# List operands by nine token tiles, a routing in smaller parts, and scales copied on GpSimd

## The chip, the cores and the metric

The kernel runs on one core of a Trainium2 chip. The metric is the device time of one execution in microseconds (us); of several runs the median counts. Engines are called as the profile calls them: PE (TensorE matmul), PEld (its weight loads), DVE (VectorE), ACT (ScalarE), POOL (GpSimd) and SP (SyncE, which issues most DMAs).

## The reference

Attention over pooled queries feeds a mixture of eight experts, of which each token uses one.

```python
# q, k, v: 8 batches x 8 heads x 1152 x 64, float32
q_pool = q.reshape(B, H, S // 2, 2, D).mean(axis=3)          # 576 queries
scores = scale * np.matmul(q_pool, k.transpose(0, 1, 3, 2))
scores = scores - np.max(scores, axis=-1, keepdims=True)
attn = np.exp(scores)
attn = attn / (np.sum(attn, axis=-1, keepdims=True) + 1e-09)
x = np.matmul(attn, v)                                       # to 4608 tokens x 512
...
logits = x @ w_gate + modality_bias[modality_id]
e_idx = np.argmax(logits, axis=1)
gate_w = probs[np.arange(N), e_idx]                          # probs = softmax(logits)
for e in range(8):
    mask = e_idx == e
    out[mask] = gate_w[mask, None] * (np.maximum(x[mask] @ w1[e], 0) @ w2[e])
```

## The kernel before

**Attention** treats 32 pairs, numbered 0 to 31; a pair is one head of two neighbouring batches, and its two members are heads j = 0 and 1. A pair takes 18 steps, and the order of every engine's work is written out by hand: a loop over 576 steps calls small generators in a fixed order (`ORD`), `at` hangs a piece of work on a step, `later` puts it some steps on, and `later_end` puts it at a step's end. Every engine then works through its own list in that order and stops only where an operand is not there yet, so an engine may be ahead of the steps of the others.

The first half of a pair's work is done one or two pairs ahead:

- GpSimd pools the queries (`split_q`, line 603, tile `rawq`), casts them to float16 (line 610, `qh`) and takes three remainders (line 638, `lo`: the first of the queries, the other two of the keys, which wait for ScalarE's casts at line 622, `hi`).
- `maxpass` finds an upper bound of each query's scores: 18 matmuls of 512 columns and nine of 128 write to a pool of three PSUM tiles (`pm`, lines 771 and 779), and VectorE reduces each to one number per query (lines 772 and 780). A matmul of this kind can start only when the reduction of the tile three back is through.
- `square`, `power` and `scales` (lines 684 to 705) find a power of two from the values' sum of squares. `scales` runs at step 1 of the pair before: VectorE writes `half`, the two factors `sc`, and then the same number twice more, into the routing's `scales` and into `both` (line 698).
- GpSimd scales the values into `VH` in two pieces (line 725) at steps 3 and 4 of the pair before, VectorE makes the shifted copy `VS` (line 735) and the low parts `vl` (line 723).

The second half: `scores` makes the score matmuls (lines 833 and 834) and their exponentials on ScalarE (line 835, 24 for a pair). The lower halves of the exponentials' 32-bit words are turned into `Pl` (line 816 on ScalarE for two thirds, line 818 on VectorE for 576 columns); `pv` multiplies both by the values (lines 886 to 888). `evac` divides by the row sums (lines 904 to 909), and `split_x` (line 862) splits the result for the gate's logits, which odd pairs multiply (line 258).

**Routing.** After every eight pairs a quarter of the tokens (a group of nine tiles of 128) is complete. `route` then adds the logits up, finds the best expert and its probability, and counts by ten small matmuls how many tokens before this one chose the same expert. It is a generator that runs beside the attention: it is called once a step, and `yield n` lets it rest for n steps. `RS = 2` sets most of these rests.

**The first list.** When three groups are routed (in pair 26), `first_blocks`, `place` and `listing` sort their tokens into six blocks of 256, so that the experts can start as soon as the attention ends. `operands` builds, for three tiles of tokens at a time, a one-hot matrix of the lane (`ol`, line 471) and two products of a one-hot of the column (`o` at line 476, `r` at lines 478 and 479); nine matmuls for a group then write the list (line 498). In the pairs from `P_LIST` = 26 on, a third of VectorE's lower halves is done by ScalarE instead.

**Experts** come after pair 31, from about 754 us on: blocks of 256 tokens, w1 and w2 split into two float16 parts each, on PE without a break; the fourth group's routing and the second list run beside their first blocks.

Of the kernel before, what the change touches and what calls it, by code (L numbers as in the profile page):

```python
# [9 lines left out]
F32 = mybir.dt.float32  # L10
F32R = mybir.dt.float32r
F16 = mybir.dt.float16
BF16 = mybir.dt.bfloat16
# [9 lines left out]
P = 128  # L23
# [6 lines left out]
D = 64  # L30
# [12 lines left out]
T_LIST = -127  # L43
RS = 2
SLOW_P = 1
# [109 lines left out]
class Router:  # L155
# [11 lines left out]
    def setup(self, ids, w_gate, bias):  # L167
# [20 lines left out]
        nc.gpsimd.memset(self.on, 1.0)  # L188
        self.ie = self.iota("ie", E)
        self.lane16 = con.tile([P, P], BF16, name="lane16")  # L190
        nc.gpsimd.tensor_copy(self.lane16, self.iota("lane", P))
# [75 lines left out]
    def route(self, g, eng):  # L267

        nc, sm = self.nc, self.sm
        while self.added[g] < H // 2:  # L270
# [15 lines left out]
        yield RS + 1  # L286
# [3 lines left out]
        yield RS  # L290
# [6 lines left out]
        yield RS  # L297
# [5 lines left out]
        yield RS  # L303
        sx = sm.tile([P, NT], F32, name="sx")
        nc.vector.tensor_reduce(sx, w, op=ALU.add, axis=AX.X)
# [5 lines left out]
        nc.vector.reciprocal(ts2[:, 1:2], ts2[:, 0:1])  # L311
# [3 lines left out]
        eng.dma_start(out=self.xs[g * NT * P:(g + 1) * NT * P, DM:XW].rearrange("(t p) d -> p t d", p=P), in_=gt)  # L315
        yield RS
# [3 lines left out]
        nc.tensor.matmul(pr[:, 0:NT], self.up, oh16, start=True, stop=False, skip_group_check=True)  # L320
        for s in range(NT):
            nc.tensor.matmul(pr[:, s + 1:], self.on, oh16[:, s:s + 1].broadcast_to([P, NT - s, E]), start=False, stop=s == NT - 1,
                             skip_group_check=True)
# [5 lines left out]
        self.base = nb  # L329
        yield RS  # L330
        nc.gpsimd.tensor_tensor(pos, pos, oh, op=ALU.mult)
        yield RS
        nc.vector.tensor_reduce(self.pos[:, ts], pos, op=ALU.add, axis=AX.X)
# [29 lines left out]
    def first_blocks(self):  # L363

        nc, sm = self.nc, self.sm
        full = self.con.tile([P, E], F32, name="full")
        self.up_to(self.base, full)
        yield
        cum = self.running(full.unsqueeze(1), "cumA")[:, 0]
        yield  # L370
        left = sm.tile([P, E], F32, name="left")
        nc.vector.tensor_scalar(left, cum[:, 0:E], -1.0, float(NA), op0=ALU.mult, op1=ALU.add)
        nc.vector.tensor_single_scalar(left, left, 0.0, op=ALU.max)
        self.na = self.con.tile([P, E], F32, name="na")
        nc.vector.tensor_tensor(self.na, full, left, op=ALU.min)
        yield
        nc.vector.tensor_single_scalar(cum, cum, float(NA), op=ALU.min)
        self.cumA = cum
        yield
        self.ownA = self.owners(cum, NA, "A")  # L380

# [37 lines left out]
    def place(self, nt, late):  # L419
# [11 lines left out]
        def pick(o, of):  # L431

            nc.vector.tensor_tensor(w, oh, be(of), op=ALU.mult)
# [9 lines left out]
        if late:  # L443
            yield from pick(ok, self.done)
            nc.vector.tensor_tensor(ok, self.pos[:, 0:nt], ok, op=ALU.is_ge)
            more = new("more")
            yield from pick(more, self.half)
            nc.vector.tensor_tensor(more, more, ok, op=ALU.mult)
            nc.vector.tensor_tensor(row, row, more, op=ALU.add)
        yield  # L450
        nc.vector.tensor_tensor(ok, self.pos[:, 0:nt], lim, op=ALU.is_ge if late else ALU.is_lt)
# [4 lines left out]
        lo = sm.tile([P, NTT], I32, name="loi")[:, 0:nt]  # L456
        nc.vector.tensor_single_scalar(lo, ri, P - 1, op=ALU.bitwise_and)
        nc.vector.tensor_single_scalar(ri, ri, 7, op=ALU.logical_shift_right)
# [3 lines left out]
        nc.vector.tensor_copy(self.hi, ri)  # L462
        nc.vector.tensor_single_scalar(self.hi, self.hi, -float(2 * T // P), op=ALU.add)

    def operands(self, g, n, out):

        nc, sm = self.nc, self.sm
        for q in range(3):
            ts = slice(g * NT + 3 * q, g * NT + 3 * q + 3)
            ol = sm.tile([P, 3, P], BF16, name=f"ol{q}", bufs=1 + self.lag)  # L470
            nc.vector.tensor_tensor(ol, self.lo[:, ts].unsqueeze(2).broadcast_to([P, 3, P]), self.lane16.unsqueeze(1).broadcast_to([P, 3, P]),
                                    op=ALU.is_equal)
            yield SLOW
            o = sm.tile([P, 3, n], F32, name=f"o{n}")
            r = sm.tile([P, 3, 2, n], BF16, name=f"r{n}_{q}", bufs=1 + self.lag)
            nc.vector.tensor_tensor(o, self.hi[:, ts].unsqueeze(2).broadcast_to([P, 3, n]), self.col[:, 0:n].unsqueeze(1).broadcast_to([P, 3, n]),
                                    op=ALU.is_equal)
            nc.vector.tensor_tensor(r[:, :, 0], o, self.tile1[:, ts].unsqueeze(2).broadcast_to([P, 3, n]), op=ALU.mult)
            nc.vector.tensor_scalar(r[:, :, 1], o, self.part, None, op0=ALU.mult)
            out.append((ol, r))  # L480
            yield SLOW

    def listing(self, groups, n, acc):

        nc, ops = self.nc, []
        for g in range(groups + self.lag):
# [7 lines left out]
            if g >= 0:  # L494
                pm = self.pm(4)[:, 0:2 * n].rearrange("p (w n) -> p w n", w=2)
                for t in range(NT):
                    ol, r = ops[g][t // 3]
                    nc.tensor.matmul(pm, ol[:, t % 3], r[:, t % 3], start=t == 0, stop=t == NT - 1)
# [21 lines left out]
    def first_list(self):  # L520

        for _ in self.first_blocks():
            yield 2
        for _ in self.place(3 * NT, False):
            yield 2
        yield T_LIST
# [12 lines left out]
def attention(tc, ctx, att, ident, npairs, xpool, on_two, on_split, on_scale, jobs, side, set_pm, started, ahead, hip):  # L539
# [153 lines left out]
    def scales(p, pt):  # L693
# [102 lines left out]
    def scores(p, j, r):  # L796
# [9 lines left out]
        s["P", j, r] = (word(F16, 1), Pl, i % NR)  # L806
        lows = LOWS_LAST if p == npairs - 1 else LOWS_LIST if p >= P_LIST else LOWS if p else LOWS0
        lows = lows[i % len(lows)]
# [672 lines left out]
```

## Time and profile before

| | |
|---|---|
| time, median of 3 runs (lowest to highest) | 1164.33 us (1164.32 to 1165.66) |
| time of the profiled execution | 1162.89 us |
| its span, first to last instruction | 1161.2 us |
| granted TensorE clock, mean over the span | 0.996 |
| first exponential of pair 0, of pair 3, end of pair 31's last | 18.2, 100.5, 753.0 us |

The profile comes from one execution. Its page gives each engine's busy time. The view of windows gives the same for chosen stretches; the stretches used here begin and end where the first exponential of a pair starts, so one row is one pair. The timeline lists instructions in order of time: start and length in us, engine, line, operation, output<-input, and in square brackets how long the engine stood idle before it and what ended that. Neighbouring instructions of one kind are merged in a row (`x2`). A few per cent of the matmul records can be missing.

### The profile page before, as it was taken

Reading aid. Unit: us, or ns where it says so; the run is one execution under the profiler, and the core shown is the slowest. Engines: PE = TensorE matmul, PEld = TensorE weight load, DVE = VectorE, ACT = ScalarE, POOL = GpSimd, SP = SyncE. Lnnn points to the kernel's source line nnn. Section 1 sums busy time; section 2 is a strip of 40 time slices with the busy share of each in tenths; the row PEclk is TensorE's granted clock in tenths of the full one; section 3 lists DMA queues with packets and bytes.
Section 4 is the critical chain, followed back from the end, with each engine's and each line's share of the span. In section 5 each row is a group of like instructions: output and inputs, shape, how many; then the busy total and the mean of one; then the engine's idle time right before and its main releaser. Section 6 shows DMA issues by size and latency. Waiting matters only on the chain. (4 is left out here: it accounts for less than half of the span.)

```text
span 1161.2 us, 36622 instructions
## 1 busy us (share of the span) xinstructions
PE 1109.2 (96%) x14962; PEld 814.1 (70%) x14962; DVE 986.0 (85%) x2021; ACT 920.7 (79%) x1469; POOL 414.0 (36%) x394
## 2 busy tenths in 40 slices
PE   5989999999999999999999999999999999999995
PEld 2767777777777777777777677767676676766763
DVE  6888999999999999999999999788997667566671
ACT  5879999998999998999999999866566656565561
POOL 7843443444435344444443342123122121221201
PEclk9999999999999999999999999999999999999998
DMA  7667758767668668678678563599989999999970
GB/s 226 171 167 171 175 159 203 166 166 184 162 166 193 175 165 179 165 165 195 160 174 183 144 139 85 173 291 267 254 283 280 322 263 278 281 280 287 269 227 22
DMA packets 175569, 232.66 MB, mean 200 GB/s; under 512 B 92351, under 2 KB 126799, under 8 KB 175392
## 3 DMA queue, kind: packets, MB, share of 16 engines
q1 hardware_dynamic: 169254, 210.45, 70.3%
q0 software_dynamic: 6128, 19.78, 6.0%
q8 instruction: 119, 1.95, 0.7%
q14 instruction: 58, 0.48, 0.1%
q10 hardware_dynamic: 10, 0.00, 0.0%
HBM read 146.11 MB, written 19.18 MB: 142 GB/s over the span
## 5 line engine op out<-in xcount | busy, mean ns | idle before, releaser
L835 ACT ACTIVATE Pe<-psc 128x432 int32<-128x432 f32 x768 | 379.1, 526 | 51.7 <-PE psc L834 42.7
L772 DVE TENSOR_REDUCE mp<-pm 128x1 f32<-128x512 f32 x566 | 370.9, 683 | 18.4 <-PE pm L771 11.4
L886 PE MATMUL xp<-VH,Pe 128*128 128x65 f16 x2880 | 373.2, 193 | 0.0
L888 PE MATMUL xp<-VS,Pl 128*128 128x65 f16 x2880 | 372.5, 193 | 0.4 <-DVE Pl L818 0.4
L887 PE MATMUL xp<-vl,Pe 128*128 128x64 f16 x2880 | 371.2, 192 | 0.0
L887 PEld LDWEIGHTS <-Pe 128*128 128x128 f16 x2880 | 267.6, 98 | 87.8
L834 PE MATMUL psc<-B 65*128 65x432 f16 (+2 forms) x1152 | 305.6, 288 | 4.6 <-DMA B<-mr 4.3
L886 PEld LDWEIGHTS <-Pe 128*128 128x128 f16 x2880 | 272.1, 98 | 52.6 <-issue 15.3
L833 PE MATMUL psc<-B 128*128 128x432 f16 (+2 forms) x1152 | 305.0, 287 | 3.3 <-ACT Pe L835 3.0
L888 PEld LDWEIGHTS <-Pl 128*128 128x128 f16 x2880 | 266.5, 97 | 0.6 <-DVE Pl L818 0.5
L816 ACT ACTIVATE Pl<-Pe 128x1152 f16<-128x1152 uint16 x196 | 223.3, 1140 | 6.2
L771 PE MATMUL pm<-hi,QB 128*128 128x512 f16 x566 | 215.2, 382 | 11.7 <-DVE mp L772 8.3
L725 POOL TENSOR_SCALAR VH<-rawv,sc 128x512 f16<-128x512 f32 (+1 forms) x60 | 103.9, 1742 | 174.1 <-PE psc L834 72.8
L638 POOL TENSOR_TENSOR lo<-rawk,hi 128x576 f16<-128x576 f32 (+1 forms) x68 | 87.4, 1288 | 187.3 <-ACT hi L622 144.4
L1222 PE MATMUL ph<-xpart,w1l 128*128 128x256 f16 x544 | 148.3, 273 | 0.0
L1220 PE MATMUL ph<-xpart,w1h 128*128 128x256 f16 x544 | 148.3, 273 | 0.0
L1221 PE MATMUL ph<-xpart,w1h 128*128 128x256 f16 x544 | 148.3, 273 | 0.0
L834 PEld LDWEIGHTS <-B 65*128 65x128 f16 x1152 | 113.1, 98 | 28.6 <-issue 5.3
L833 PEld LDWEIGHTS <-B 128*128 128x128 f16 x1152 | 112.8, 98 | 8.2 <-issue 3.0
L1226 DVE SCALAR_TENSOR_TENSOR hl<-ph,hh 128x512 f16<-128x512 f32 x72 | 49.6, 689 | 74.5 <-ACT hh L1225 74.4
L1268 PE MATMUL po<-w2h,hl 128*128 128x512 f16 x296 | 112.2, 379 | 0.0
L1267 PE MATMUL po<-w2l,hh 128*128 128x512 f16 x296 | 112.2, 379 | 0.0
(264 smaller groups left out, 1843.3 us busy)
## 6 DMA issues: line engine op xcount, KB each, us to landing
w2r<-in_w_dram SPq DMA_DIRECT2D x76, 512.0 KB
w1r<-in_w_dram SPq DMA_DIRECT2D x72, 512.0 KB
rawv<-in_att_dram SPq DMA_DIRECT2D x32, 576.0 KB
B<-hi SPq DMA_DIRECT2D x128, 144.0 KB
rawq<-in_att_dram SPq DMA_DIRECT2D x31, 576.0 KB
rawk<-in_att_dram SPq DMA_DIRECT2D x31, 576.0 KB
B<-qh SPq DMA_DIRECT2D x128, 72.0 KB
B<-lo SPq DMA_DIRECT2D x64, 144.0 KB
```

What stands on the lines that cost most here:

```text
L771: nc.tensor.matmul(pm, QB[p % 2][:, u], s["hi"][:, t * 512:(t + 1) * 512], start=True, stop=True)
L772: nc.vector.tensor_reduce(mp[:, u, t:t + 1], pm, op=ALU.max, axis=AX.X)
L816: nc.scalar.activation(low, rest, AF.Copy, scale=LOW)
L833: nc.tensor.matmul(o, b1[:, ks], b1[:, qs], start=True, stop=False, skip_group_check=True)
L834: nc.tensor.matmul(o, b2[:, ks], b2[:, qs], start=False, stop=True, skip_group_check=True)
L835: nc.scalar.activation(Pe[:, D + x0:D + x1], pt, AF.Exp, scale=1.0 / 16)
L886: nc.tensor.matmul(out, Ph[:, qs], vh[:, c, j, 0:D + 1], start=c == 0 and g == 0, stop=False, skip_group_check=True)
L887: nc.tensor.matmul(out[:, 0:D], Ph[:, qs], vl[:, c, j], start=False, stop=False, skip_group_check=True)
L888: nc.tensor.matmul(out, Pl[:, qs], vs[:, c, j, 0:D + 1], start=False, stop=c == NKC - 1, skip_group_check=True)
L1220: nc.tensor.matmul(o, hi[:, c, fs], xh[:, :, c], start=c == 0, stop=False)
L1221: nc.tensor.matmul(o, hi[:, c, fs], xl[:, :, c], start=False, stop=False)
L1222: nc.tensor.matmul(o, lo[:, c, fs], xh[:, :, c], start=False, stop=c == 3)
```

## The change

- `scales` no longer writes `scales` and `both` on VectorE. A new function `keep`, one step later, copies them from `sc` on GpSimd.
- `route` is split into more parts. Its rests are four steps for the first two groups (`RS = (4, 4, 2, 2)`). Five of VectorE's operations for a group go: a compare and a cast are folded into their neighbours, and three small ones go to GpSimd.
- `first_blocks` is written out with a rest of one step after every operation or two, `place` has more rests and two operations fewer (three more in the second list).
- `operands` builds the column's one-hot and its two products for all nine tiles of a group at once, between the three lane matrices. A group's rests go from six to five.
- In pairs 28 to 30 all of the lower halves of 576 columns are VectorE's again (pairs 26 and 27 keep their third on ScalarE).

The core of the diff:

```diff
-RS = 2
+PL = 2
+RS = (4, 4, 2, 2)
...
-P_LIST = 26
-LOWS_LIST = (((0, 1152, 'A', 2), (1152, 1728, 'D', 3)), ((0, 1152, 'A', 2), (1152, 1728, 'D', 3)), ((0, 1152, 'A', 2), (1152, 1728, 'A', 3)))
+P_LIST = {26: 0, 27: 0}
+LOWS_LIST = [tuple(((0, 1152, 'A', 2), (1152, 1728, e, 3)) for e in x) for x in ('DDA', 'DA', 'A')]
...
         nc.scalar.activation(w, lg, AF.Exp)
-        nc.vector.tensor_single_scalar(w2, lg, 0.0, op=ALU.is_ge)
         key = big[1][:, 0]
-        nc.vector.scalar_tensor_tensor(key, w2, -float(E), be(self.ie), op0=ALU.mult, op1=ALU.add)
+        nc.vector.scalar_tensor_tensor(key, lg, 0.0, be(self.ieE), op0=ALU.is_ge, op1=ALU.mult)
...
-        oh = big[1][:, 1]
+        oh = sm.tile([P, NT, E], BF16, name="oh16")
         nc.vector.tensor_tensor(oh, key, bc(kmin), op=ALU.is_equal)
-        oh16 = sm.tile([P, NT, E], BF16, name="oh16")
-        nc.vector.tensor_copy(oh16, oh)
-        nc.vector.tensor_single_scalar(self.exp[:, ts], kmin, float(E), op=ALU.add)
-        yield RS
+        yield 1
+        nc.gpsimd.tensor_scalar(self.exp[:, ts], kmin, float(E), None, op0=ALU.add)
+        yield rs
         nc.vector.tensor_reduce(sx, w, op=ALU.add, axis=AX.X)
-        nc.vector.tensor_single_scalar(sx, sx, EPS, op=ALU.add)
...
-        nc.vector.tensor_single_scalar(ts2[:, 0:1], ts2[:, 0:1], 1.0 / XSC, op=ALU.mult)
+        yield 1
+        nc.gpsimd.tensor_scalar(sx, sx, EPS, None, op0=ALU.add)
+        nc.gpsimd.tensor_scalar(ts2[:, 0:1], ts2[:, 0:1], 1.0 / XSC, None, op0=ALU.mult)
+        yield 1
         nc.vector.reciprocal(ts2[:, 1:2], ts2[:, 0:1])
...
-            nc.vector.tensor_tensor(w, oh, be(of), op=ALU.mult)
+            nc.vector.scalar_tensor_tensor(w, oh, float(TB), be(of), op0=ALU.mult, op1=ALU.mult)
             yield
             nc.vector.tensor_reduce(o, w, op=ALU.add, axis=AX.X)
-            nc.vector.tensor_single_scalar(o, o, float(TB), op=ALU.mult)
...
     def operands(self, g, n, out):
-        for q in range(3):
...
-            yield SLOW
-            o = sm.tile([P, 3, n], F32, name=f"o{n}")
...
+        rows(0)
+        yield SLOW
+        o = sm.tile([P, NT, n], F32, name=f"o{n}")
+        nc.vector.tensor_tensor(o, self.hi[:, ts].unsqueeze(2).broadcast_to([P, NT, n]), self.col[:, 0:n].unsqueeze(1).broadcast_to([P, NT, n]),
+                                op=ALU.is_equal)
+        yield SLOW
+        rows(1)
+        yield SLOW
+        nc.vector.tensor_tensor(r[:, 0], o, self.tile1[:, ts].unsqueeze(2).broadcast_to([P, NT, n]), op=ALU.mult)
+        nc.vector.tensor_scalar(r[:, 1], o, self.part, None, op0=ALU.mult)
+        yield SLOW
+        rows(2)
+        yield SLOW
...
-        on_scale(p, lambda o: power_of(o, half, 1, 49))
         if p % 2 == 0:
             s["both"] = xpool.tile([P, 1], I32, name="both", bufs=3)
+        later(1, lambda: keep(p, sc))
+
+    def keep(p, sc):
+
+        on_scale(p, lambda o: nc.gpsimd.tensor_copy(o, sc[:, 1:2]))
         r = slice(p % 2 * D, (p % 2 + 1) * D)
-        power_of(st[p - p % 2]["both"][r], half[r], 1, 49)
+        nc.gpsimd.tensor_copy(st[p - p % 2]["both"][r], sc[r, 1:2])
```

Two places in the order of instructions. The first is GpSimd's list around the turn from one pair to the next, in the stretch before the first routing. Before, with the pooling (`rawq`) of the pair after next directly behind the last remainders (`lo`):

```order
L638 TENSOR_TENSOR lo<-rawk,hi 128x576 x2
L603 TENSOR_TENSOR rawq<-rawq 128x576
L725 TENSOR_SCALAR VH_125<-rawv,sc 128x8x64
L725 TENSOR_SCALAR VH_125<-rawv,sc 128x10x64
L610 CAST qh<-rawq 128x576
L638 TENSOR_TENSOR lo<-rawq,qh 128x576
```

The same stretch in the changed kernel, whose line numbers are larger by 30 to 34:

```order
L668 TENSOR_TENSOR lo<-rawk,hi 128x576 x2
L738 COPY scales<-sc 128x1
L740 COPY both<-sc 64x1
L633 TENSOR_TENSOR rawq<-rawq 128x576
L759 TENSOR_SCALAR VH_125<-rawv,sc 128x8x64
L759 TENSOR_SCALAR VH_125<-rawv,sc 128x10x64
L640 CAST qh<-rawq 128x576
L668 TENSOR_TENSOR lo<-rawq,qh 128x576
```

The two copies, which need `sc` of the running pair's step 1, now stand ahead of the pooling, and the pooling stays ahead of `VH`.

The second is VectorE's list in pair 10, where the first group's routing runs; `L772`/`L806` is the reduction of `maxpass`, `L818`/`L852` the lower half, `L723`/`L757` the values' low part. Before:

```order
L299 TENSOR_TENSOR wide_5691<-wide_5691,kmin 128x72
L301 CAST oh_5987<-wide_5691 128x72
L302 TENSOR_SCALAR exp<-kmin 128x9
L772 TENSOR_REDUCE mp<-pm 128x1 x2
L818 TENSOR_SCALAR Pl_116<-Pe_115 128x576
L305 TENSOR_REDUCE sx<-wide_5690 128x9
L306 TENSOR_SCALAR sx<-sx 128x9
L309 TENSOR_REDUCE ts_6047<-scales 128x1
L310 TENSOR_SCALAR ts_6047<-ts_6047 128x1
L311 RECIPROCAL ts_6047<-ts_6047 128x1
L312 RECIPROCAL gt<-sx 128x9
L313 TENSOR_SCALAR gt<-gt,ts_6047 128x9
```

The same operations in the changed kernel:

```order
L305 TENSOR_REDUCE sx<-wide_5694 128x9
L308 TENSOR_REDUCE ts_6377<-scales 128x1
L806 TENSOR_REDUCE mp<-pm 128x1 x2
L852 TENSOR_SCALAR Pl_116<-Pe_115 128x576
L806 TENSOR_REDUCE mp<-pm 128x1 x2
L757 SCALAR_TENSOR_TENSOR vl<-rawv,sc,VH_127 128x512
L313 RECIPROCAL ts_6377<-ts_6377 128x1
L314 RECIPROCAL gt<-sx 128x9
L315 TENSOR_SCALAR gt<-gt,ts_6377 128x9
```

Seven operations in a row became two and three, with the pair's own work between them, and the one-hot (`oh`, line 299, now line 300), without the cast behind it, stands eleven rows ahead of the first of these instead of five.

More of the change, by code (lines that the diff above doesn't have):

```diff
@@ L319, in route @@
         pr = self.pm(4)[:, 0:(NT + 1) * E].rearrange("p (t e) -> p t e", e=E)
[L320 removed]
+        nc.tensor.matmul(pr[:, 0:NT], self.up, oh, start=True, stop=False, skip_group_check=True)
         for s in range(NT):
[L322 removed]
+            nc.tensor.matmul(pr[:, s + 1:], self.on, oh[:, s:s + 1].broadcast_to([P, NT - s, E]), start=False, stop=s == NT - 1,
                              skip_group_check=True)
@@ L366, in first_blocks @@
         full = self.con.tile([P, E], F32, name="full")
-        self.up_to(self.base, full)
+        i = sm.tile([P, E], I32, name="cnti")
+        nc.vector.tensor_copy(i, self.base)
         yield
-        cum = self.running(full.unsqueeze(1), "cumA")[:, 0]
+        nc.vector.tensor_single_scalar(i, i, TB.bit_length() - 1, op=ALU.logical_shift_right)
+        yield
+        nc.vector.tensor_copy(full, i)
+        yield
+        w = sm.tile([P, 1, E + 1, E], F32, name="wcumA")
+        nc.vector.tensor_tensor(w[:, 0], full.unsqueeze(1).broadcast_to([P, E + 1, E]), self.before, op=ALU.mult)
+        yield
+        cum = self.con.tile([P, E + 1], F32, name="cumA")
+        nc.vector.tensor_reduce(cum, w[:, 0], op=ALU.add, axis=AX.X)
         yield
@@ L455, in place @@
         nc.vector.tensor_copy(ri, row)
-        lo = sm.tile([P, NTT], I32, name="loi")[:, 0:nt]
+        yield
+        lo, hi = (sm.tile([P, NTT], I32, name=f"{x}i")[:, 0:nt] for x in ("lo", "hi"))
         nc.vector.tensor_single_scalar(lo, ri, P - 1, op=ALU.bitwise_and)
-        nc.vector.tensor_single_scalar(ri, ri, 7, op=ALU.logical_shift_right)
+        nc.vector.tensor_single_scalar(hi, ri, 7, op=ALU.logical_shift_right)
+        yield
         self.lo = sm.tile([P, NTT], BF16, name="lof")[:, 0:nt]
@@ L467, in operands, with rows @@
         nc, sm = self.nc, self.sm
-        for q in range(3):
-            ts = slice(g * NT + 3 * q, g * NT + 3 * q + 3)
-            ol = sm.tile([P, 3, P], BF16, name=f"ol{q}", bufs=1 + self.lag)
-            nc.vector.tensor_tensor(ol, self.lo[:, ts].unsqueeze(2).broadcast_to([P, 3, P]), self.lane16.unsqueeze(1).broadcast_to([P, 3, P]),
-                                    op=ALU.is_equal)
-            yield SLOW
-            o = sm.tile([P, 3, n], F32, name=f"o{n}")
[L475 to L481, printed above, removed]
+        ts = slice(g * NT, (g + 1) * NT)
+        r = sm.tile([P, 2, NT, n], BF16, name=f"r{n}", bufs=1 + self.lag)
+        ols = [sm.tile([P, 3, P], BF16, name=f"ol{q}", bufs=1 + self.lag) for q in range(3)]
+        out.append((ols, r))
+        def rows(q):
+            t3 = slice(g * NT + 3 * q, g * NT + 3 * q + 3)
+            nc.vector.tensor_tensor(ols[q], self.lo[:, t3].unsqueeze(2).broadcast_to([P, 3, P]), self.lane16.unsqueeze(1).broadcast_to([P, 3, P]),
+                                    op=ALU.is_equal)
+        rows(0)
[11 more added lines that the diff above has]
+        yield SLOW
     def listing(self, groups, n, acc):
@@ L496, in listing @@
                 for t in range(NT):
-                    ol, r = ops[g][t // 3]
-                    nc.tensor.matmul(pm, ol[:, t % 3], r[:, t % 3], start=t == 0, stop=t == NT - 1)
+                    ols, r = ops[g][0]
+                    nc.tensor.matmul(pm, ols[t // 3][:, t % 3], r[:, :, t], start=t == 0, stop=t == NT - 1)
                 yield 1
```

42 lines of the change are left out of this document (26 added, 16 removed).

## The prediction

> **What bounds the kernel.** The page shows PE as the busiest engine.
>
> ```profile
> PE 1109.2 (96%) x14962; PEld 814.1 (70%) x14962; DVE 986.0 (85%) x2021; ACT 920.7 (79%) x1469; POOL 414.0 (36%) x394
> ```
>
> Shares over the span say little, so I read windows, one for each pair. Columns: stretch, length, then busy time of PE, PEld, DVE, ACT and POOL, the granted clock, DMA. The rows are pairs 10, 14, 15, 16 and 26 to 29.
>
> ```profile
> 255.66:279.67 24.01, 22.16 (x381) 16.97 (x380) 23.30 (x59) 21.26 (x37) 10.22 (x9) 1.00 0.81 184
> 346.21:367.84 21.63, 21.63 (x376) 16.78 (x373) 21.09 (x45) 20.82 (x39) 9.60 (x7) 1.00 0.90 186
> 367.84:389.97 22.13, 22.13 (x391) 17.17 (x390) 21.02 (x48) 20.89 (x37) 9.26 (x7) 1.00 0.61 171
> 389.97:411.60 21.63, 21.28 (x365) 16.33 (x362) 20.73 (x45) 20.82 (x39) 9.60 (x7) 1.00 0.89 180
> 613.91:638.21 24.30, 22.88 (x392) 17.52 (x391) 23.64 (x67) 22.03 (x39) 10.21 (x9) 1.00 0.83 176
> 638.21:662.81 24.60, 22.75 (x388) 17.25 (x385) 24.04 (x63) 22.42 (x40) 9.27 (x7) 1.00 0.53 146
> 662.81:687.16 24.35, 22.46 (x377) 17.21 (x377) 23.89 (x58) 22.67 (x39) 10.13 (x7) 1.00 0.68 135
> 687.16:710.97 23.81, 22.80 (x398) 17.43 (x395) 23.42 (x58) 22.26 (x39) 8.19 (x6) 1.00 0.36 90
> ```
>
> Pairs 14 and 16 take 21.63 us each and PE is busy for all 21.63 of the first (records are missing in the second): an ordinary even pair stands at PE's floor. An odd pair (15) takes 22.13, with logits on top, PE again busy throughout. Pair 10, with a routing, takes 24.01, 2.4 more than the floor, and VectorE is busy for 23.30 of it. Pairs 26 to 29, with the third routing and the first list, sum to 97.06 against 87.52 for two even and two odd ones: 9.5 more, VectorE busy for 94.99. So VectorE bounds the special pairs, and PE the ordinary ones, VectorE being close behind (21.09 of 21.63). What the change can gain lies in two routings of 2.4 and a list of 9.5; what it can lose lies in the 23 ordinary pairs, where a stall of PE is never made good.
>
> **The change, part by part.**
>
> *Scales' copies.* The timeline of VectorE in pair 16, then PE's matmul that matters later:
>
> ```profile
> 391.70 0.21 DVE L698 TENSOR_SCALAR sc<-half 128x1 int32<-128x1 int32 x2
> 391.83 0.14 DVE L698 TENSOR_SCALAR scales<-half 128x1 int32<-128x1 int32 x1
> 391.99 0.15 DVE L698 TENSOR_SCALAR both<-half 64x1 int32<-64x1 int32 x1
> 392.23 1.46 DVE L772 TENSOR_REDUCE mp<-pm 128x1 f32<-128x512 f32 x2
> 393.72 0.95 DVE L818 TENSOR_SCALAR Pl<-Pe 128x576 f16<-128x576 uint16 x1
> ...
> 398.34 0.46 DVE L818 TENSOR_SCALAR Pl<-Pe 128x576 f16<-128x576 uint16 x1
> ...
> 399.69 0.88 DVE L723 SCALAR_TENSOR_TENSOR vl<-rawv,sc,VH 128x640 f16<-128x640 f32 x1
> 400.48 0.68 DVE L772 TENSOR_REDUCE mp<-pm 128x1 f32<-128x512 f32 x1
> ```
> ```profile
> 401.25 0.38 PE L771 MATMUL pm<-hi,QB 128*128 128x512 f16 x1
> ```
>
> VectorE loses 0.14 + 0.15 = 0.29 us a pair. In an ordinary pair I count this as nothing: the pair is at PE's floor, and the next reduction starts 0.09 after `both` ends. GpSimd's side costs more. Its timeline:
>
> ```profile
> 384.94 1.41 POOL L603 TENSOR_TENSOR rawq<-rawq 128x576 f32<-128x576 f32 x1
> 392.02 3.44 POOL L725 TENSOR_SCALAR VH<-rawv,sc 128x512 f16<-128x512 f32 x2 [5.67 <-PE xp L888]
> ...
> 396.15 1.28 POOL L638 TENSOR_TENSOR lo<-rawq,qh 128x576 f16<-128x576 f32 x1
> 400.10 1.61 POOL L638 TENSOR_TENSOR lo<-rawk,hi 128x576 f16<-128x576 f32 x1 [2.67 <-ACT hi L622]
> ...
> 406.95 1.41 POOL L603 TENSOR_TENSOR rawq<-rawq 128x576 f32<-128x576 f32 x1
> ```
>
> Today the pooling runs ahead in the pair before (384.94, 1.41 long), and GpSimd then idles 5.67 until `sc` is there. In the changed list the copies stand ahead of the pooling and need that `sc`. So the pooling can start only after 392.02, and `VH`, `qh` and the first `lo` follow it: later by 1.41 and two copies. No copy of one column stands in the trace; the nearest is this.
>
> ```profile
> L314 POOL COPY gt<-ts 128x9 f32<-128x9 f32 x4 | 0.8, 192 | 7.7 <-DVE ts L311 7.7
> ```
>
> Two take between 0.1 (nearly overlapped) and 0.38; I take 0.25. The first `lo` moves from 396.15 by 1.66 to about 397.8, and ends at 399.1.
>
> There VectorE's own work now meets it, and the two engines do not run such operations side by side. Pair 16's third pooling row and VectorE's next lower half show it, and pair 27 shows what follows:
>
> ```profile
> 407.75 0.93 DVE L818 TENSOR_SCALAR Pl<-Pe 128x576 f16<-128x576 uint16 x1
> ```
> ```profile
> 647.91 1.28 POOL L638 TENSOR_TENSOR lo<-rawk,hi 128x576 f16<-128x576 f32 x1 [3.06 <-ACT hi L622]
> 648.26 1.62 DVE L723 SCALAR_TENSOR_TENSOR vl<-rawv,sc,VH 128x640 f16<-128x640 f32 x1
> ...
> 651.02 0.38 PE L771 MATMUL pm<-hi,QB 128*128 128x512 f16 x1 [1.05 <-DVE mp L772]
> ```
>
> The lower half that began 0.80 into the pooling took 0.93 instead of 0.46: it ended 0.32 after the pooling (408.68 against 408.36). The `vl` that began 0.35 into `lo` took 1.62 instead of 0.88, ending 0.69 after it (649.88 against 649.19), and PE then stood 1.05 for a reduction.
>
> Now the same for pair 16. The lower half at 398.34 finds `lo` running until 399.1 and ends at 399.4 instead of 398.80: 0.6 late. So `vl` comes at 400.3, after the second `lo`, which ScalarE releases at 400.10 as before; that `lo` is then 1.28 long, ends at 401.4, and `vl` at 402.1 instead of 400.57. The reduction behind it ends at 402.7 instead of 401.16, and PE's matmul of 401.25, which started 0.09 after that end, has to wait some 1.4. In return the pooling no longer meets the lower half of 407.75 (0.47 less on VectorE, of which I give PE 0.3). I take 1.1 for an even pair, with 0.3 and 1.4 as bounds. The lower half of 393.72 meets the first piece of `VH` instead of the second: nothing.
>
> For odd pairs, pair 15:
>
> ```profile
> 375.96 0.46 DVE L818 TENSOR_SCALAR Pl<-Pe 128x576 f16<-128x576 uint16 x1
> ...
> 377.31 0.88 DVE L723 SCALAR_TENSOR_TENSOR vl<-rawv,sc,VH 128x640 f16<-128x640 f32 x1
> ```
> ```profile
> 373.70 1.28 POOL L638 TENSOR_TENSOR lo<-rawq,qh 128x576 f16<-128x576 f32 x1
> 378.06 1.28 POOL L638 TENSOR_TENSOR lo<-rawk,hi 128x576 f16<-128x576 f32 x1 [3.07 <-ACT hi L622]
> ```
>
> `lo` would run from 375.4 to 376.6, the lower half ends 0.55 late, `vl` starts at 377.9, still ahead of 378.06. VectorE's idle 1.11 takes most of the delay; I take 0.15, bounds 0 and 1.1 (if `vl` comes second, as in pair 27). Sum over even pairs 4 to 24, 11 x 1.1 = 12.1, and odd pairs 3 to 25, 12 x 0.15 = 1.8: **+13.9**.
>
> The Trainium skill ("SBUF — State Buffer", section "SBUF: two separate sides") says that VectorE and GpSimd arbitrate for one port pair, and that whichever starts first holds it for the whole instruction. The rows of `lo` and the pooling agree with it. With `VH` they don't: the lower half of 393.72 ended at 394.67, while `VH` ran to 395.46. By it the sum would be some 11 higher (a rival, below); by the row of `VH` it stands.
>
> *Routing.* Pair 10's burst, first and last of seven operations in a row:
>
> ```profile
> 260.60 0.22 DVE L305 TENSOR_REDUCE sx<-wide 128x9 f32<-128x72 f32 x1
> ...
> 261.63 0.23 DVE L313 TENSOR_SCALAR gt<-gt,ts 128x9 f32<-128x9 f32 x1
> ```
>
> It holds VectorE for 1.26 and is now cut into two and three operations, six steps later and two apart; the cast and additions go. PE's ten small matmuls and three operations move to pair 11, which has little room for them. I take 1.25 gained of each 2.4, bounds 0 and 2, for two routings: **-2.5** (their pairs pay the 1.1 above).
>
> *List.* VectorE's groups in pairs 28 and 29:
>
> ```profile
> L818 DVE TENSOR_SCALAR Pl<-Pe 128x576 f16<-128x576 uint16 x8 | 4.1, 510 | 0.1
> L471 DVE TENSOR_TENSOR ol<-lof,lane 128x384 bf16<-128x384 bf16 x6 | 3.3, 545 | 0.0
> ...
> L478 DVE TENSOR_TENSOR r<-o,tile 128x36 bf16<-128x36 f32 x6 | 1.6, 262 | 0.2
> ...
> L479 DVE TENSOR_SCALAR r<-o,part 128x36 bf16<-128x36 f32 x6 | 1.5, 242 | 0.0
> L476 DVE TENSOR_TENSOR o<-hif,col 128x36 f32<-128x36 f32 x6 | 1.1, 185 | 0.0
> ```
> ```profile
> 651.49 0.37 DVE L433 TENSOR_TENSOR wide<-wide,cumA 128x216 f32<-128x216 f32 x1
> ```
>
> Two groups cost 1.6 + 1.5 + 1.1 = 4.2 for 18 narrow operations. They become six of 108 columns, between 0.19 and 0.37 each (36 and 216 columns); at 0.28 that is 1.7, so 2.5 less, and 0.5 (one lane matrix) slips into pair 30: -3.0. Scales: 4 x 0.29 = -1.2. The third routing and `place` lose six operations of about 0.18: -1.1. Four lower halves come back to pairs 28 and 29, 4 x 0.51 = +2.0; ScalarE, relieved of them, was not what these pairs waited for (22.67 of 24.35). Together **-3.3**; VectorE is busy 95.0 of 97.06 there, so I count it whole, with bounds -6 (fewer meetings with GpSimd) and 0 (more). In pair 30 two more lower halves meet slack.
>
> *Experts.* They wait for nothing of this; the second list takes fewer operations beside blocks that PE fills: 0, +-0.5.
>
> Sum: 13.9 - 2.5 - 3.3 = **+8.1**. The profiled execution took 1162.89, 1.44 less than the median 1164.33, so the forecast is 1164.33 + 8.1 = **1172.4** us.
>
> **Rivals.**
>
> *Faster: the delay is taken up.* PE loses nothing if `vl` still comes before the second `lo`, or if a free `pm` tile covers it. The point is 400.10 against my 400.3: 0.2 less delay of the first `lo` turns it. Then only -2.5 - 3.3 = -5.8 are left: 1158.5. For it: even pairs already hide two lower halves of 0.93 to 0.95. Against it: pair 27, where 0.35 was enough.
>
> *Both parities, or a longer hold.* If copies take 0.45 instead of 0.25, the odd `vl` comes second too: 12 x 1 more, 1184.
>
> *A hold by `VH` to its end.* If a `VH` piece keeps VectorE out until it ends, the lower half at 393.72, which now meets the first piece, ends some 1.0 later in 11 even pairs, and everything behind it: 1183. The row of `VH` above speaks against it. This is what the rule of the Trainium skill's "SBUF — State Buffer" of above would make of the turn.
>
> *Half of it:* the meetings cost even pairs 0.5, or VectorE makes good the rest: 13.9 becomes some 6.5, and all comes to 1165.
>
> **How the numbers follow.** Forecast 0.47 (1167 to 1179), faster rival 0.32 (1155 to 1161), half 0.10, both parities 0.08, the hold by `VH` 0.03. The range 1155 to 1179 leaves out the last two, and the ends of others; the forecast's own is 1167 to 1179. About 0.2%, 2.3 us, is what a measurement here can tell from no change: below 1162.0 the faster rival, 0.32; within, the half case, 0.10; above, 0.58.
>
> **What would show it.** Right: windows of even pairs near 22.7 with a PE wait on `mp` of about 1; GpSimd's pooling after the copies; `vl` of 640 columns above 1.2 in even pairs. Routing pairs near 24, pairs 26 to 29 near 94. Wrong: even pairs still at 21.63, or a pooling that runs before `sc`; then the faster rival holds. If odd pairs exceed 23, it is the other.

## The result, and the profile after

The changed kernel took 1185.25 us (median of 4 runs, 1181.04 to 1186.63) beside 1164.78 for the kernel before (four runs by now): a ratio of 1.0169, with a 95% interval of 1.0142 to 1.0196. That is 20 us slower, in the direction forecast and more than twice the 8.1 forecast. The profiled execution took 1181.04, 18.15 above that of before.

The page shows an engine that works as much as before over a longer time:

```profile
PE 1112.3 (94%) x14962; PEld 815.8 (69%) x14962; DVE 991.0 (84%) x1895; ACT 923.0 (78%) x1463; POOL 435.8 (37%) x472
```

The windows by pair, in the order of those of before (pairs 10, 14, 15, 16, then 26 to 29):

```profile
260.48:283.50 23.02, 21.74 (x366) 16.48 (x363) 22.42 (x53) 21.40 (x39) 11.22 (x13) 1.00 0.80 168
352.26:375.58 23.32, 21.07 (x361) 16.10 (x358) 21.53 (x42) 21.30 (x39) 9.95 (x9) 1.00 0.79 163
375.58:398.71 23.13, 23.13 (x407) 17.98 (x404) 21.78 (x46) 21.23 (x35) 9.98 (x9) 1.00 0.62 172
398.71:423.42 24.71, 21.09 (x361) 16.12 (x358) 21.53 (x42) 21.30 (x39) 9.96 (x9) 1.00 0.78 162
634.48:658.53 24.05, 22.77 (x395) 17.61 (x394) 22.51 (x58) 22.24 (x39) 11.99 (x14) 1.00 0.79 190
658.53:684.11 25.58, 23.09 (x395) 17.66 (x392) 24.82 (x57) 22.48 (x39) 9.73 (x9) 1.00 0.47 129
684.11:707.24 23.13, 21.38 (x363) 16.23 (x360) 21.95 (x52) 21.34 (x38) 9.91 (x9) 1.00 0.65 138
707.24:731.44 24.20, 22.67 (x395) 17.43 (x392) 23.91 (x54) 21.34 (x38) 10.25 (x9) 1.00 0.36 89
```

Even pair 14 grew from 21.63 to 23.32 and 16 from 21.62 to 24.71, with PE idle for 2.25 and 3.62 of them (in pair 14, 1.1 of it in waits for a reduction and 1.1 in one for the maxima's row); odd pair 15 grew from 22.14 to 23.13. The routing pair 10 fell by 1.0. Pairs 26 to 29 sum to 96.96, as before (97.06). Cut into triples of steps (by the scores' exponentials, 24 in a pair), pairs 3 to 25 lost 23.1 in all; of that, steps 9 to 11 of the nine even pairs without a routing lost 8.8, and the last triple of even pairs with the first of odd ones 13.2. Outside, pairs 0 to 2 won 2.0, 30 and 31 won 1.9.

PE's waits name the two places. Columns: total, times, longest; first before, then after.

```profile
PE pm L771 <- DVE mp L772: 8.3, 14, 1.1
...
PE psc L834 <- DMA B<-mr: 4.3, 7, 1.2
```
```profile
PE pm L805 <- DVE mp L806: 18.4, 30, 1.7
PE psc L868 <- DMA B<-mr: 11.3, 12, 2.5
```

The first is the one forecast, the wait for a reduction. The second, for the maxima's row that SyncE sends into `B`, stood in no term of the sum. Here is the first in pair 14: GpSimd's timeline, then VectorE's.

```profile
354.26 0.19 POOL L738 COPY scales<-sc 128x1 int32<-128x1 int32 x1 [7.07 <-DVE sc L728]
354.51 0.18 POOL L740 COPY both<-sc 64x1 int32<-64x1 int32 x1
354.77 1.41 POOL L633 TENSOR_TENSOR rawq<-rawq 128x576 f32<-128x576 f32 x1
356.16 3.63 POOL L759 TENSOR_SCALAR VH<-rawv,sc 128x512 f16<-128x512 f32 x2
359.75 0.66 POOL L640 CAST qh<-rawq 128x576 f16<-128x576 f32 x1
360.49 1.40 POOL L668 TENSOR_TENSOR lo<-rawq,qh 128x576 f16<-128x576 f32 x1
362.39 1.28 POOL L668 TENSOR_TENSOR lo<-rawk,hi 128x576 f16<-128x576 f32 x1 [0.50 <-ACT hi L652]
```
```profile
360.28 0.46 DVE L852 TENSOR_SCALAR Pl<-Pe 128x576 f16<-128x576 uint16 x1
360.66 1.54 DVE L769 TENSOR_SCALAR VS<-VH 128x1152 f16<-128x1152 f16 x1
362.13 0.68 DVE L806 TENSOR_REDUCE mp<-pm 128x1 f32<-128x512 f32 x1
362.73 1.62 DVE L757 SCALAR_TENSOR_TENSOR vl<-rawv,sc,VH 128x640 f16<-128x640 f32 x1
```

GpSimd idles 7.07 for `sc`, then copies, then pools. `lo` begins at 360.49, 8.23 into the pair, where it began 6.18 into pair 16 before (396.15 in 389.97). The lower half begins 0.21 ahead of `lo` and escapes; `VS`, next, needs 1.54 where a free one takes 0.46 (0.45 in e10, below), and ends 0.31 after `lo`. So `vl` starts at 362.73, behind the second `lo` (362.39), and takes 1.62 instead of 0.88.

And the second place: SyncE's queue in pair 14, before and after (issue time, and how long the issue held the queue).

```profile
352.32 1.10 SPq L573 DMA_DIRECT2D QB<-qh  x2
353.52 0.53 SPq L593 DMA_DIRECT2D rawv<-in_att_dram  x1
...
358.25 4.39 SPq L870 DMA_TRANSPOSE xt<-x  x2
362.74 0.80 SPq L757 DMA_DIRECT2D B<-mr  x1
```
```profile
360.43 1.70 SPq L603 DMA_DIRECT2D QB<-qh  x2
362.23 0.53 SPq L623 DMA_DIRECT2D rawv<-in_att_dram  x1
...
365.06 6.60 SPq L904 DMA_TRANSPOSE xt<-x  x2
371.75 0.79 SPq L791 DMA_DIRECT2D B<-mr  x1
```
```profile
375.20 0.34 PE L868 MATMUL psc<-B 65*128 65x432 f16 x1 [1.10 <-DMA B<-mr]
```

`qh` comes 2.1 later in the pair, so the queries' moves and the two large loads behind them on the same queue do too. The two transposes then hold the queue for 6.60 instead of 4.39, and the row goes out 19.5 into the pair instead of 16.5. PE's first scores of pair 15 wait 1.10 for it. Over the nine even pairs from 4 to 24 without a routing, the row went out 16.0 to 17.6 into the pair before (17.1 on average) and 18.5 to 19.6 after (19.0). Even before, PE waited for it in five of these nine, by 0.34 to 0.95: this path had no slack.

One of the waits came with a further loss. After the longest, 2.49 at the end of pair 16, the granted clock was 0.50 for 3.42 us in pair 17 (423.87 to 427.29); at half the clock that is up to 1.7 us, an estimate, within the 13.2.

### The profile page after: what moved, and what is told of

The parts are those of the page before. It is cut to its first block, busy times and chain, and to the rows that moved or that the text cites. A ratio compares the mean times of both kernels' runs of the same rounds, so it can differ in the third digit from the quotient of the medians.

```text
span 1179.3 us, 36588 instructions
## 1 busy us (share of the span) xinstructions
PE 1112.3 (94%) x14962; PEld 815.8 (69%) x14962; DVE 991.0 (84%) x1895; ACT 923.0 (78%) x1463; POOL 435.8 (37%) x472
## 5 line engine op out<-in xcount | busy, mean ns | idle before, releaser
L869 ACT ACTIVATE Pe<-psc 128x432 int32<-128x432 f32 x768 | 384.0, 526 | 68.5 <-PE psc L868 55.4
L806 DVE TENSOR_REDUCE mp<-pm 128x1 f32<-128x512 f32 x566 | 372.1, 684 | 30.3 <-PE pm L805 24.1
L868 PE MATMUL psc<-B 65*128 65x432 f16 (+2 forms) x1152 | 305.8, 288 | 11.5 <-DMA B<-mr 11.3
L805 PE MATMUL pm<-hi,QB 128*128 128x512 f16 x566 | 215.3, 383 | 20.3 <-DVE mp L806 18.4
L850 ACT ACTIVATE Pl<-Pe 128x1152 f16<-128x1152 uint16 (+1 forms) x190 | 219.3, 1154 | 6.0
L852 DVE TENSOR_SCALAR Pl<-Pe 128x576 f16<-128x576 uint16 (+1 forms) x194 | 106.0, 547 | 7.8 <-ACT Pe L869 7.0
L1300 PE MATMUL po<-w2h,hh 128*128 128x512 f16 x296 | 112.2, 379 | 0.0
```

Source lines behind the costliest of these rows:

```text
L805: nc.tensor.matmul(pm, QB[p % 2][:, u], s["hi"][:, t * 512:(t + 1) * 512], start=True, stop=True)
L806: nc.vector.tensor_reduce(mp[:, u, t:t + 1], pm, op=ALU.max, axis=AX.X)
L850: nc.scalar.activation(low, rest, AF.Copy, scale=LOW)
L868: nc.tensor.matmul(o, b2[:, ks], b2[:, qs], start=False, stop=True, skip_group_check=True)
L869: nc.scalar.activation(Pe[:, D + x0:D + x1], pt, AF.Exp, scale=1.0 / 16)
```

## The experiments

Each run is compared with runs of the kernel before on its own chip, whose medians were 1162.5 to 1163.8; where two runs are compared with each other, it is by how far each lies above that median (the changed kernel: 20.5). The theory after the traces: the copies' place makes GpSimd's turn late, and that costs twice, in the meetings on VectorE and on SyncE's queue. The rivals: the routing and list parts cost it; the copies cost it wherever they stand; or the two waits are one loss.

**e1, the copies back on VectorE.**

```diff
-        on_scale(p, lambda o: nc.gpsimd.tensor_copy(o, sc[:, 1:2]))
+        on_scale(p, lambda o: nc.vector.tensor_copy(o, sc[:, 1:2]))
...
-        nc.gpsimd.tensor_copy(st[p - p % 2]["both"][r], sc[r, 1:2])
+        nc.vector.tensor_copy(st[p - p % 2]["both"][r], sc[r, 1:2])
```

> The changed kernel with the two copies of the scale given back to VectorE, nothing else undone. Theory (the copies stand ahead of GpSimd's pooling, so its whole turn comes late; late, it meets VectorE's copies in even pairs, and delays the maxima's row on SyncE's queue in both parities): the lateness goes, pairs 4 to 25 fall by some 24 us and pairs 26 to 29 by 2 to 4; 1157 (1153 to 1161). Rival (the new routing and list parts, which put matmuls and small operations into other pairs, cost the time): it stays above 1176.

Measured: 1164.22, ratio 0.9996 (0.9982 to 1.0011). All 20 us go with these two lines; steps 9 to 11 of the even pairs are back at 3.57 to 3.58 from 4.55. But it came out 7 above the 1157 expected: what is left of the change gains nothing that can be measured.

**e2, the copies alone moved, in the kernel before.** The edit is the change's own hunk from `scales` to `keep`.

> The kernel before with the two copies alone moved to GpSimd, in the changed kernel's place. Theory: the loss of 24 us in pairs 4 to 25 appears here, and 2 to 4 more in pairs 26 to 29, since nothing is gained by routing and list: 1190 (1183 to 1196), slower than the changed kernel or as slow. Rival (routing and list cost): within 2 us of the kernel before, 1165.

Measured: 1192.39, ratio 1.0246 (1.0225 to 1.0267). Steps 9 to 11 lost the same 8.8 in nine pairs; the last triple of even and the first of odd pairs lost 11.0. That is 28.6 above the kernel before, against 20.5 for the changed kernel. With e1, the copies at this place are shown to be the whole loss, and the rest of the change to give some 8 back where the turn is late (in the profiled runs, 4.7 of it in pairs 26 to 29 and 3.6 in pairs 0 to 2, which vary between runs).

**e3, the copies on GpSimd, but late.**

```diff
-        later(1, lambda: keep(p, sc))
+        later(10, lambda: keep(p, sc))
```

> The changed kernel with the copies still on GpSimd, but issued nine steps later, in its idle time behind the second lower part of the keys. Theory (only their place ahead of the pooling costs): as e1 or a little faster, since VectorE is spared the copies: 1156 (1152 to 1160). Rival (copies on GpSimd cost wherever they stand, by their own time and the port): half or more of the loss stays, above 1170.

Measured: 1168.34, ratio 1.0035 (1.0018 to 1.0051). Not the copies but their place cost four fifths. Steps 9 to 11 are at 3.57 again. What stays is on the queue: `qh` ends 6.36 into an even pair instead of 6.08, the row goes out at 17.2 to 19.1 (17.9 on average) in the nine even pairs instead of 16.1 to 18.2 (17.2) in e1, and PE waits 13.1 for it instead of 7.9. By these numbers, 0.7 on that queue is enough to be measured.

**e4, the row by ScalarE's queue**, meant to take away the second loss alone.

```diff
-            (nc.sync if p or u0 else nc.scalar).dma_start(out=B2...
+            (nc.scalar if p or not u0 else nc.sync).dma_start(out=B2...
```

> The changed kernel with the maxima's row sent by ScalarE's queue instead of SyncE's, where it stands behind two transposes; the late turn of GpSimd stays. Theory of two separate losses (meetings on VectorE, some 1.0 in an even pair; the row's lateness, 0.3 to 2 at the turn from one pair to the next): PE's waits for the row (11.3 in 12) go, those for the reduction (18.4 in 30) stay: 1172 (1167 to 1178). Rival (one loss: PE has to wait for the late maxima anyway, and the row's wait only shows it): above 1181.

Measured: 1185.68, ratio 1.0189 (1.0163 to 1.0215), which the rival foretold, but not for its reason. PE's waits for the row fell from 11.3 to 4.5 and those for the reduction stayed at 18.4, as the theory had it. The gain was eaten by a new cost, seen in ScalarE's timeline:

```profile
373.26 0.66 ACT L652 CAST hi<-rawk 128x576 f16<-128x576 f32 x1
373.81 0.73 ACTq L791 DMA_DIRECT2D B<-mr  x1
374.59 0.53 ACT L869 ACTIVATE Pe<-psc 128x432 int32<-128x432 f32 x1 [0.67 <-DVE rs L938]
```

Issuing the row holds ScalarE for 0.73 in this pair, and steps 12 to 14 grow by 0.77 (3.70 to 4.47). Over pairs 3 to 25 these steps took 18 more than in the changed kernel, and the turns from even to odd pairs gave back 15. By its time the run decides nothing.

**e9, without the second transpose**, a cleaner way to the same end. The kernel leaves this transpose out and computes the logits' lower part from the upper one's, so its output is another one.

```diff
-            turn_part(p, 1, xl)
-            on_split(p // 2, s["xt"] if p < npairs - 1 else (xh, xl), ...
+            on_split(p // 2, [s["xt"][0]] * 2 if p < npairs - 1 else (xh, xl), ...
```

> The changed kernel without the second transpose of each two pairs (the logits' lower part is then computed from the upper one's transpose), so that the maxima's row follows the first transpose on SyncE's queue; GpSimd's turn and VectorE's order stay. Theory of two losses: PE's waits for the row (11.3 in 12) nearly go, steps 9 to 11 of even pairs stay at 4.55: 1185 less 10 to 14, 1172 (1168 to 1177). Rival (one loss, the row's wait only shows work that is late anyway): above 1181.

Measured: 1169.76, ratio 1.0064 (1.0043 to 1.0084): 7.3 above the kernel before, so 13.2 less than the changed kernel. The turns alone, in the profiled run, gave back 12.3.

```profile
PE pm L805 <- DVE mp L806: 18.4, 30, 1.7
...
PE psc L868 <- DMA B<-mr: 2.5, 4, 1.1
```

The row's wait goes, the reduction's stays whole, steps 9 to 11 stay at 4.55. So the row's lateness costs something that the meeting does not explain, and more than the meeting; what the second transpose itself cost as traffic, which this run takes away with it, is in the 13.2 and was not separated.

**e10, the other loss taken away**: the queries' lower part behind the first of the keys'.

```diff
-T_LO = (-23, -26, -17, -19, -26, -17, -23)
+T_LO = (-23, -25, -17, -19, -26, -17, -23)
```

> The changed kernel with GpSimd's lower part of the queries one step later, behind the first lower part of the keys; its turn is as late as in the changed kernel. Theory (the meeting decides: the scaled copy VS meets the queries' lower part and takes 1.54 instead of 0.46, so the lower values come behind the keys' lower part): VS falls to 0.46, the lower values start ahead of the keys' part, steps 9 to 11 of even pairs fall to 3.58, the row stays late: 1185 less 11 to 14, 1172 (1168 to 1177). Rival (the late scaled values or maxima stall PE, the port only shows it): steps 9 to 11 stay near 4.5, above 1181.

Measured: 1198.52, ratio 1.0304 (1.0279 to 1.0328): 36.0 above the kernel before, 15.5 slower than the changed kernel where 13 less was expected. The meeting went as foretold (pair 14, VectorE and then GpSimd):

```profile
368.83 0.45 DVE L769 TENSOR_SCALAR VS<-VH 128x1152 f16<-128x1152 f16 x1
...
369.80 0.88 DVE L757 SCALAR_TENSOR_TENSOR vl<-rawv,sc,VH 128x640 f16<-128x640 f32 x1
```
```profile
370.56 1.28 POOL L668 TENSOR_TENSOR lo<-rawk,hi 128x576 f16<-128x576 f32 x1 [2.00 <-ACT hi L652]
371.80 1.29 POOL L668 TENSOR_TENSOR lo<-rawq,qh 128x576 f16<-128x576 f32 x1
```

`VS` takes 0.45 and `vl` 0.88 with GpSimd's turn as late as ever, steps 9 to 11 are at 3.58, and PE's waits for reductions fall from 18.4 to 6.0: the meeting is shown to be the cause of the first loss. But the load of `rawq` waits for that part of `lo`, and on SyncE it now goes out right ahead of the transposes:

```profile
373.12 0.81 SPq L618 DMA_DIRECT2D rawq<-in_att_dram  x1
374.02 6.25 SPq L904 DMA_TRANSPOSE xt<-x  x2
380.37 0.80 SPq L791 DMA_DIRECT2D B<-mr  x1
```

PE's waits for the row went from 11.3 to 32.1 (14 times). The expectation had the row "stay late", and priced no change of it. By the trace three things add up here. The row goes out 0.7 later in the nine even pairs (19.6 on average instead of 19.0). PE, which no longer loses 0.98 in steps 9 to 11, comes to the scores that much sooner and only waits there: with the row this late, taking the meeting away alone gains nothing. And eight of these waits, 2.4 to 3.8 long, each came with a stretch in which the granted clock was 0.50; these last 37.5 us in sum, which at half the clock costs up to 19 us, an estimate. With the waits of 1.3, 2.2 and 1.7 in pairs 10, 12 and 18 none came. Pairs 14 and 15, with the clock behind PE, PEld, DVE, ACT and POOL:

```profile
360.42:384.62 24.20, 21.07 (x361) 16.09 (x358) 20.25 (x42) 20.91 (x38) 9.81 (x9) 0.98 0.82 161
384.62:410.44 25.82, 25.82 (x408) 19.79 (x406) 21.87 (x46) 21.34 (x36) 10.02 (x9) 0.89 0.53 151
```

**e7 and e8, the row ahead of the second transpose**, in the changed kernel and in e1.

```diff
-XL = 3
+XL = 4
```

> The changed kernel with the split of the outputs' lower part one step later, so that SyncE sends the maxima's row ahead of the second transpose; GpSimd's turn stays late. Theory of two losses: the row's waits (11.3) nearly go, those for the reduction (18.4) stay, steps 9 to 11 of even pairs stay at 4.55, the last steps of even and the first of odd pairs go to 4.02 and 2.87 to 3.5: 1175 (1171 to 1179). Rival (one loss): above 1181.

> e1 (copies on VectorE) with the maxima's row ahead of the second transpose. If PE's waits for the row (7.9 in 9 in e1) are a loss of their own, most of them go: 1158 (1155 to 1161), below both kernels. If they only stand for logits or value work that is late anyway: 1163 to 1165, as e1.

Measured: 1199.98, ratio 1.0296 (1.0266 to 1.0326), and 1181.58, ratio 1.0155 (1.0129 to 1.0182). Both missed by 17 to 25. The row's waits did fall (to 3.0 and 1.9), but the split, 0.81 on VectorE in e1, meets GpSimd's last `lo` one step later and takes 1.45 in the median. Here it is ahead of e8's pair 14:

```profile
347.92 1.65 DVE L896 SCALAR_TENSOR_TENSOR x<-x,sc,x 128x576 f16<-128x576 f32 x1
...
347.68 1.28 POOL L668 TENSOR_TENSOR lo<-rawk,hi 128x576 f16<-128x576 f32 x1 [3.94 <-ACT hi L652]
```

That pushes `sc` of the next pair from 1.72 to 2.65 into it. `VH` waits for `sc`, so e8 made GpSimd's work behind it late again, by 0.92, without any copy on GpSimd. So e8 shows how near the two orders lie. Two of its pairs, 14 and 20, have `sc` at the same place, and differ in a lower half that is held up beside `VH` in the one (1.05) and not in the other (0.46). VectorE in both pairs, then GpSimd:

```profile
358.66 1.05 DVE L852 TENSOR_SCALAR Pl<-Pe 128x576 f16<-128x576 uint16 x1
...
364.72 1.85 DVE L757 SCALAR_TENSOR_TENSOR vl<-rawv,sc,VH 128x640 f16<-128x640 f32 x1
...
497.23 0.46 DVE L852 TENSOR_SCALAR Pl<-Pe 128x576 f16<-128x576 uint16 x1
...
502.71 0.88 DVE L757 SCALAR_TENSOR_TENSOR vl<-rawv,sc,VH 128x640 f16<-128x640 f32 x1
```
```profile
364.61 1.28 POOL L668 TENSOR_TENSOR lo<-rawk,hi 128x576 f16<-128x576 f32 x1 [2.15 <-ACT hi L652]
...
503.18 1.54 POOL L668 TENSOR_TENSOR lo<-rawk,hi 128x576 f16<-128x576 f32 x1 [1.85 <-ACT hi L652]
```

In pair 14 `vl` starts 0.11 after the second `lo`, takes 1.85, and steps 9 to 11 take 4.55. In pair 20 it starts 0.47 ahead of it, takes 0.88 (`lo` then takes 1.54 instead of 1.28), and they take 3.57. One start order decides 0.98.

**e5 and e6, the routing and the list alone**, hunks of the change put into the kernel before.

> The kernel before with the routing part alone (its spacing, the fused key, the additions on GpSimd). As forecast: 1.25 gained in each of two routing pairs and nothing lost beside them, pairs 10+11 from 46.28 to 45.0, 1162. By the windows of e1 (the operations, moved to steps 9 to 11, meet GpSimd's work there): pairs 10+11 and 18+19 near 45.6, so 1.3 in all, 1163 (1161 to 1165). Rival (the third routing, at its narrow spacing with two more waits, gives it back in pairs 25 to 27): within 0.5 of the kernel before.

> The kernel before with the list over nine tiles alone, and its rule for the lower halves. As forecast: pairs 26 to 29 fall by 1 to 2 of their 97.06 (the 3.3 less the scales' and the routing's share), 1163. By the windows of e1: VectorE has less to do there, but the lower halves that come back to it and the listing's bunching leave pair 29 longer by what pair 28 is shorter: 97.0 to 97.6, no change, 1164 to 1165. Rival (the lower halves come back without need): slower by over 1, above 1165.5.

Measured: 1168.70, ratio 1.0041 (1.0028 to 1.0055), and 1163.93, ratio 1.0007 (0.9992 to 1.0021). The routing's two pairs gained as e1's did (24.0 to 23.0 each, with 0.3 given back in the pair behind). But its third group lost 5.8 in pairs 26 to 29, most of it in pairs 27 and 28:

```profile
639.59:665.75 26.16, 23.27 (x400) 17.84 (x399) 25.67 (x62) 22.76 (x38) 9.57 (x7) 1.00 0.45 128
665.75:693.64 27.89, 23.88 (x373) 17.95 (x370) 26.45 (x63) 22.50 (x39) 9.33 (x7) 0.94 0.50 118
```

VectorE is busy for 25.67 and 26.45 there (24.04 and 23.89 before): `vl` starts 2.6 and 2.0 behind the second `lo` (0.35 and 1.0 before). It starts after that `lo` has ended and takes 0.87, so this is no meeting: VectorE's own list is late there. The clock was 0.94 in pair 28, so a part of its 27.89 may be PE's. In the whole change (e1) these two pairs take 24.1 and 23.5, so the other parts undo that; which of them was not tried. The list won 1.4 in pairs 26 to 29 and gave 0.7 back in 30 and 31.

**e11 and e12, the split one step earlier** (`XL = 2`), in the kernel before, and there with the routing part for its first two groups alone.

> The kernel before with the split of the outputs' lower part one step earlier, so that the second transpose and behind it the row are issued some 0.4 earlier on SyncE. If the row's waits (4.3 in 7) are a loss of their own at its edge: most go, 1160 to 1162. If VectorE's order costs more than that (as it did in the other direction in e8, by 17): 1166 or more. Neither: 1164.

> The kernel before with the routing part for its first two groups alone (the third keeps its spacing and gets no further waits) and the earlier split of e11. Theory: 1.3 gained at pairs 10 and 18, the 5 that e5 lost in pairs 26 to 28 not lost, and what e11 gives: 1159 to 1162. Rival (the additions on GpSimd or the fused key cost the third group's pairs whatever the spacing): 1164 to 1168.

Measured: 1171.34, ratio 1.0070 (1.0052 to 1.0089), and 1170.20, ratio 1.0065 (1.0043 to 1.0086). No better kernel came of it. PE's waits for the row fell to 3.3 and 1.9, but those for the maxima `m`, which the split now stands ahead of, rose from 3.9 in 7 times to 14.8, in 23 times (e11) and 25 (e12). Of all versions run, none is below the kernel before by more than its interval.

## Why the prediction was wrong

**The first half of the mechanism was right.** The copies stand ahead of the pooling and wait for `sc`. Counted from `sc`, `VH` came 1.87 and the first `lo` 2.06 late in even pairs, 1.6 in odd ones (1.66 forecast; in even pairs the copies begin 0.25 apart instead of overlapping, and `VH` took 0.2 more beside a lower half). `vl` fell behind the second `lo` in every even pair from 4 to 24, and in odd ones (but for pair 3, which lost 1.3 in steps 9 to 11) it stayed ahead, while in most of them the lower half met the first `lo` (0.92 instead of 0.46). The victim in even pairs was `VS` and not the lower half, which escaped by 0.21; `vl` came 0.77 late (0.6 forecast). Per even pair this cost 0.98 of PE's time (1.1 forecast), so 8.8 in the nine pairs against 12.1 forecast for eleven; the two routing pairs, counted with them, would have met anyway: they show 4.56 in e1 too.

**The step that failed** is the sum for the late turn, "+13.9". It follows the late `qh` to `lo` and the meeting on VectorE, and puts what `qh` releases on SyncE at nothing, without a reason: a step that is moved moves its DMAs. There `qh` is the head of an ordered queue: moves, loads, transposes, row. The turns from even to odd pairs lost 13.2 in the profiled run, for which the sum had no term; e9, in which the row goes out without waiting for the second transpose, took 13.2 off the time. "I take 0.15" for odd pairs was near, for what it was meant for: their steps 3 to 17 lost 2.4 in all (1.8 forecast), of which pair 3 alone 1.3. So the size came near the rival "both parities" (1184) by luck and by another way: its `vl` came second in one odd pair alone.

**Routing, -2.5.** The burst did cost its pairs 1.28 each, in steps 3 to 5, and this came back whole (4.82 and 4.85 to 3.55). But the operations, six steps later, bring `vl` behind the second `lo` in that pair: 0.74 lost in steps 9 to 11 (3.81 to 4.55), which needed no copies (e1). With 0.3 in the pairs behind, 1.3 was left of 2.5 in e1.

**List, -3.3.** VectorE did become freer, by 1.80 and not 3.3: its busy time over pairs 26 to 29 fell from 94.99 to 93.19. In pairs 28 and 29 six operations of 108 columns took 0.26 to 0.27 each (0.28 taken) and the lower halves cost 1.8 more (2.0 taken), but the lane matrices took 0.77 each instead of 0.55. The pairs' time fell by 0.84 there and rose by 0.73 in 26 and 27. "I count it whole" failed: of the 1.80, 0.1 reached the time. PE's waits for reductions in these four pairs stayed (5.3 in sum, 4.7 before); which order of operations causes each was not tried. The late turn's own cost in pairs 26 to 29 was left out of the sum as well: e2 shows 4.6 there, but in the change as a whole there is none to be seen (96.96, and 97.4 in e1).

**Not forecast:** pairs 0 to 2 won 2.0 and pairs 30 and 31 won 1.9, in the profiled run. For pairs 0 to 2 no experiment tells why, and in the kept traces this stretch came out from 2.2 shorter to 1.8 longer than in the kernel before, the 1.8 with an edit of the routing alone (e5): the 2.0 may not be the change's.

**The hold of the port.** By the runs, whichever of the two starts first keeps the other waiting to about its end, for `lo`, the pooling, `vl`, `VS` and the split: `vl` 0.11 behind `lo` took 1.85 and ended 0.68 after it, `lo` 0.41 behind `vl` took 1.61 instead of 1.28 and ended 1.14 after it (pair 16 before: 400.10 and 399.69). The rule of the Trainium skill's "SBUF — State Buffer" (section "SBUF: two separate sides") agrees with these rows. The rival that `VH` holds to its end did not come: in pair 15 of the changed kernel a lower half that began 0.44 into `VH` took 0.56 (380.27 to 380.83, `VH` 379.83 to 383.25), and in e8's pair 14 one took 1.05 (358.66 to 359.71) while `VH` ran to 360.49. The lower half that took 0.61 in even pairs began under the pooling, ahead of `VH`; PE lost nothing at that place.

## What to carry to other kernels

An operation moved to an idle engine takes its waits along: look at what stands behind it there, and follow each of those to its consumers on every queue, the DMA queue too, before calling the move free. Where two engines share a resource by who comes first, a delay costs nothing up to a point and a fixed sum beyond it, so the margin between two starts (here 0.4 in even pairs) is the number to read, and moving one operation by a step in either direction may cost more than all it was meant to save. When two delays meet at one later point, taking away the smaller alone can be worth nothing (e10). Work taken off an engine that is 98% busy in a stage was worth almost nothing here (0.1 of 1.80).

## What had not been expected of the hardware

Issuing a small DMA of 2.2 KB held ScalarE's own instruction stream for 0.73 us (0.79 on SyncE), so a transfer moved to a computing engine's queue is paid for in its time. The issue of a transpose held SyncE for 2.03 and 1.93 us in pair 14 before, and for 4.13 and 2.38 in the changed kernel, where two loads of 576 KB had gone out 2.2 to 2.8 ahead of the first instead of 4.1 to 4.7; everything behind it on the queue waits for that. How much the loads have to do with it is not shown: with the same distances, the first one held it for 1.79 (pair 8) to 3.32 (pair 6) before. And the row, of 2.2 KB, issued at 371.75, let PE go on at 375.20 only: 3.45 on the way, beside the other transfers. Last, a wait of PE can cost more than its length: with the 2.49 of the changed kernel and with each of eight waits of 2.4 to 3.8 in e10 came a granted clock of 0.50 for 3.4 or 6.8 us.
